# Retention and a low-rank mixer on one core: half-sequence loads of q and k, one PE burst per chunk, batch 0 from q

## The chip, the core and the metric

The kernel runs on one core of one Trainium2 chip. The core has a matrix engine (PE, with its weight loads PEld), three engines for element-wise work (DVE, ACT, POOL), and SP, which here only issues DMAs. POOL issues DMAs too, besides its own work. An engine takes its instructions in order and waits at the first one whose inputs or buffers are not free. Matmuls read SBUF and write PSUM; only DVE and ACT read PSUM here. The metric is the device time of one execution in microseconds.

## The reference

Four batches, eight heads of 64, a sequence of 768. First a decayed linear attention, then a mixer: a low-rank product along the sequence, and an MLP over the channels.

```python
for t in range(S):
    state = gamma[None, :, None, None] * state + np.einsum('bhd,bhe->bhde', k[:, :, t], v[:, :, t])
    y[:, :, t] = scale * np.einsum('bhd,bhde->bhe', q[:, :, t], state)
...
x = np.ascontiguousarray(attn_out.transpose(0, 2, 1, 3)).reshape(B, S, H * D)
...
xt = x.transpose(0, 2, 1)
h = xt @ U @ V                       # U: 768 x 32, V: 32 x 768
u = x + h.transpose(0, 2, 1)
ch = np.maximum(u @ w_ch1, 0.0) @ w_ch2   # 512 -> 2048 -> 512
return (u + ch).astype(np.float32)
```

## The kernel before

Everything on PE is bf16. The sequence of a batch is cut into six chunks of 128. The decay is folded into q and v by factors, so that a chunk needs four products: its **scores** (k by q, masked to the causal half by DVE: `a`), the **mix** (`a` by v), the **query** (q by the state of the chunks before) and the **state** (k by v, added up in PSUM). Mix and query add up in one PSUM region and give x.

The order of all instructions is written by hand. Three stages follow each other:

- **Batch 0 by itself** (L672 to L737): nothing else can run on PE yet. It works in blocks of 256 rows (`cast_early`, `turn_early`, `score_early`, `state_early`, `mix_early`), with casts shared out to DVE ("D"), POOL ("P") and ACT ("A"). Then x is turned, the low-rank product is added, and the result is written to `uTs[0]` as input of the MLP (L736).
- **Preparation of batch 1** on POOL (L738 to L755): casts of q, k, v, with the loads of the weights w1, w2 and of q's second half issued between them.
- **Three weaves** (L765 to L799): `weave` lays out the MLP of batch b-1 as a list of pieces, each with a cost in us, and calls the retention of batch b and the low-rank part at given marks, shares of that list's total. A last weave has the MLP of batch 3 alone.

An MLP piece is either `up` (L463: four matmuls of w1 with `uTs`, 512 or 256 wide, into one of three PSUM banks called mlp, then a Relu by ACT or DVE into `gT`) or `down` (L486: four of the sixteen matmuls of one output chunk; after the last, DVE adds u and POOL stores it).

Around a chunk, `score4` (L356) and `mix4` (L377) are called at two marks (L760). For b > 1 `score4` also computes the state; for b = 1 k has not been loaded in its natural layout, so `natural_k` (L319) makes it on PE, and the state comes in `mix4`. Scores and query use PE as four row tiles of 32 (shape 32*128), the state as column tiles of 32 (128*32), the rest uses it whole.

After the last chunk, `lr_proj` (L411) and `lr_expand` (L421) make u, and `lr_turn` (L436) turns it into `uTs[b]`: for b < 2 by PE (L445) and ACT, for b > 1 by DMA transposes on SP (L439), one for each chunk j. The first four must have landed before the next weave's first MLP piece.

Loads: q and k that will be turned lie in one buffer each (`kin`, `qin`), filled for batch 1 by `load_half` (head by head, half a sequence) and for batches 2, 3 by `load_whole` (L107: two heads, the whole sequence, 384 KB). k and v in natural layout (below: "naturals", 256 KB a chunk) go into a ring of 19 buffers. `feed_more` (L136) issues the loads of batches 2 and 3 on SP in list order: T (q and k whole), then k and v of each chunk, as buffers come free; `pause` (L762) stops it for a while. At most eight of SP's DMAs are under way, as each waits for the one eight places before it.

Of the kernel before, what the change touches and what calls it, by code (L numbers as in the profile page):

```python
# [16 lines left out]
def kernel(  # L17
# [75 lines left out]
    n_fed, n_held, hold_feed = [0], [0], [False]  # L93
    ready = {}
    turned_in = {}
    n_cast = {b: 0 for b in range(-1, B)}

    def feed_natural(nm, b, ci):
        src = {"k": k, "v": v}[nm]
        feed.append(((nm, b, ci),  # L100
                     src[b, :, ts(ci, P), :].rearrange("h p d -> p h d")))

    def open_in(nm, b):
        turned_in[nm, b] = rinT.tile([P, 2, NCK, 256], fp32, tag=nm + "in",
                                     name=f"{nm}in_{b}")

    def load_whole(nm, b):  # L107
        open_in(nm, b)
        src = {"q": q, "k": k}[nm][b]
        for hp in (0, 2, 1, 3):  # L110
            nc.sync.dma_start(
                out=turned_in[nm, b][ds(32 * hp, 32)].rearrange(
                    "p h c x -> p (h c) x"),
                in_=src[ds(2 * hp, 2)].rearrange("h (c t j) d -> t (h c) (j d)",
                                                 c=NCK, t=32))

    def load_half(nm, half, eng, part=range(8)):
        c = ds(3 * half, 3)
        src = {"q": q, "k": k, "v": v}[nm]
        if nm != "v":  # L120
            if half == 0:
                open_in(nm, 1)
            for h in [(0, 4, 1, 5, 2, 6, 3, 7)[i] for i in part]:
                eng.dma_start(
                    out=turned_in[nm, 1][ds(32 * (h // 2), 32), h % 2, c],
                    in_=src[1, h, ts(half, 384)].rearrange(
                        "(c t j) d -> t c (j d)", c=3, t=32))
            return
        for ci in range(3 * half, 3 * half + 3):
            t = rin.tile([P, 512], fp32, tag="in", name=f"v1_{ci}")  # L130
            n_held[0] += 1
            ready["v", 1, ci] = t
            eng.dma_start(out=t.rearrange("p (h d) -> p h d", h=H),
                          in_=src[1, :, ts(ci, P)].rearrange("h p d -> p h d"))

    def feed_more():  # L136
        while n_fed[0] < len(feed) and n_held[0] < RING and not hold_feed[0]:
            key, src = feed[n_fed[0]]
            if key[0] == "T" and n_cast[key[1] - 1] < 2 * NCK:
                return  # L140
            n_fed[0] += 1
            if key[0] == "T":
                load_whole("k", key[1])
                load_whole("q", key[1])
                continue
            n_held[0] += 1
            t = rin.tile([P, 512], fp32, tag="in", name=f"in_{n_fed[0]}")
            ready[key] = t
            nc.sync.dma_start(out=t.rearrange("p (h d) -> p h d", h=H), in_=src)  # L149
# [5 lines left out]
    for b in range(2, B):  # L155
        feed.append((("T", b), None))
        for ci in range(NCK):
            feed_natural("k", b, ci)
            feed_natural("v", b, ci)
    NB = S // 256  # L160
    early = {}
    kin0 = rinT.tile([P, NB, H, P], fp32, tag="kin", name="kin_0")
    qin0 = rinT.tile([P, NB, H, P], fp32, tag="qin", name="qin_0")

    def load_early(nm, B0):
        src = {"q": q, "k": k, "v": v}[nm][0, :, ds(256 * B0, 256), :].rearrange(
            "h (t j) d -> t h (j d)", j=2)
        if nm == "v":
            early["v", B0] = []
            for f in range(2):  # L170
                t = rin.tile([P, 4, P], fp32, tag="in", name=f"v0_{B0}_{f}")
                nc.sync.dma_start(out=t, in_=src[:, ds(4 * f, 4)])
                early["v", B0].append(t)
        else:
            t = (kin0 if nm == "k" else qin0)[:, B0]
            nc.sync.dma_start(out=t, in_=src)
            early[nm, B0] = t

    for nm, B0 in ("k0", "q0", "v0", "k1", "q1", "v1", "q2", "k2", "v2"):
        load_early(nm, int(B0))  # L180
# [45 lines left out]
    def late_consts():  # L226
        nc.vector.tensor_scalar(mask, jmat, srange, None, op0=ALU.is_ge)
        nc.vector.tensor_tensor(
            pos, pos, lgt[:, None, :].to_broadcast([P, NCK, H]), op=ALU.mult)
        nc.scalar.activation(gk, pos, AF.Exp, scale=-1.0)  # L230
        for h in range(H):
            r = ds(32 * (h // 2), 32)
            nc.vector.tensor_scalar(
                posT[r, :, h % 2], posT[r, :, h % 2],
                -0.5 * math.log(D) / lg[h] - 128.0 * (h // 2), lg[h],
                op0=ALU.add, op1=ALU.mult)
        nc.scalar.activation(gqT, posT, AF.Exp)

    def causal(n):
        return mask[:, None, :].to_broadcast([P, n, P])  # L240
# [3 lines left out]
    def prep_turned(nm, b, ci, eng="P"):  # L244
        src = turned_in[nm, b][:, :, ci].rearrange("p h (a j d) -> p h a j d", a=2,
# [86 lines left out]
    def state(b, ci):  # L332
        if ci == NCK - 1:
            return
# [17 lines left out]
        ns = rmid.tile([P, 320], bf16, tag="ns", name=f"ns_{b}_{ci}")  # L352
        evac("A", ns[:, :256], st_p[:, :256])
        live["state", b, ci] = ns

    def score4(b, ci):  # L356
        if b == 1:
            natural_k(b, ci)
# [15 lines left out]
        if b > 1:  # L374
            state(b, ci)
# [457 lines left out]
```

## Time and profile before

| what | value |
|---|---|
| median of 8 runs | 234.86 us (233.65 to 235.85) |
| profiled execution, its own time | 234.14 us |
| its span in the profile | 232.3 us |
| PE busy | 212.6 us (92%) |
| DVE, ACT, POOL busy | 106.2, 78.8, 94.7 us |
| DMA moved | 34.95 MB, mean 150 GB/s |
| MLP up matmuls (L467) | 500 recorded, 89.3 us busy |
| MLP down matmuls (L492) | 385 recorded, 85.0 us busy |

The span is the time from the first to the last instruction in the profile; the difference to the execution's own time lies around it. A line such as "A L1 <- B L2: 1.5, 1, 1.5" among the waits says that engine A, at line 1, waited for what B did at line 2: in total, how often, and the longest. A timeline row has start, length, engine, line, operation, tiles (out<-in), shapes and count; a row merges equal instructions that follow each other. A few matmul records are missing from a trace.

### The profile page before, as it was taken

To read this page: it belongs to the slowest core of one execution; us is meant where nothing else is said; L and a number is where in the kernel's file an instruction comes from. 1 tells how busy PE (TensorE), PEld (TensorE's weight loads), DVE (VectorE), ACT (ScalarE), POOL (GpSimd) and SP (SyncE) were. 2 spreads that over 40 slices of the span, in tenths; PEclk is the share of its full clock that TensorE was granted. 3 is DMA by queue.
4 is the path that set the end of the run, shared out by engine and by line. 5 is a ranking of instruction groups with operands and counts; after the bars stand their busy time and mean duration, and the time that the engine had idled before them with its cause. 6 is when DMAs were issued, how large, how long until landed. Compare 5 with 4: busy or idle time off the path is not lost.

```text
span 232.3 us, 5722 instructions
## 1 busy us (share of the span) xinstructions
PE 212.6 (92%) x2402; PEld 119.4 (51%) x2430; DVE 106.2 (46%) x200; ACT 78.8 (34%) x173; POOL 94.7 (41%) x132
## 2 busy tenths in 40 slices
PE   0589699999999999999999979999999999999991
PEld 0478445657445444467444424477444444774451
DVE  5267558665534254555435155555436152222121
ACT  2474355567212127456210025555110044540000
POOL 3787159897111499911098176400101100001110
PEclk9999999999999999999999999999999999999999
DMA  7999989999999999099999932000022530001212
GB/s 180 290 291 245 232 195 224 277 208 195 235 206 215 314 235 275 24 218 205 189 242 251 254 76 45 3 1 3 3 90 71 158 90 0 3 0 47 92 62 74
DMA packets 63882, 34.95 MB, mean 150 GB/s; under 512 B 40064, under 2 KB 61952, under 8 KB 63856
## 3 DMA queue, kind: packets, MB, share of 16 engines
q1 hardware_dynamic: 57344, 23.37, 48.4%
q0 software_dynamic: 6512, 11.21, 19.9%
q8 instruction: 19, 0.31, 0.6%
q14 instruction: 7, 0.06, 0.1%
HBM read 30.90 MB, written 6.29 MB: 160 GB/s over the span
## 4 chain that ended last, share of the span: by engine, by line
PE 67%; SPq 12%; issue 9%; DMA 4%; DVE 3%; ACT 2%; POOL 1%; POOLq 0%; DVEq 0%
PE mlp L467 33%; PE mlp L492 19%; SPq L149 10%; DMA qin<-in_q_dram 2%; SPq L439 2%; PE r L396 2%; PE r L363 2%; PE mlp L566 2%; DMA uT<-u 2%; PE r L387 1%; PE st L348 1%; ACT qt L72 1%; PE r L588 1%; POOL out_dram L456 1%; PE r L424 1%
## 5 line engine op out<-in xcount | busy, mean ns | idle before, releaser
L467 PE MATMUL mlp<-uT,w1b 128*128 128x256 bf16 (+1 forms) x500 | 89.3, 325 | 2.9 <-DMA uT<-u 1.5
L492 PE MATMUL mlp<-w2b,gT 128*128 128x512 bf16 (+2 forms) x385 | 85.0, 370 | 1.0 <-issue 0.3
L474 ACT ACTIVATE gT<-mlp 128x512 bf16<-128x512 f32 (+1 forms) x88 | 42.7, 490 | 75.8 <-PE mlp L467 74.9
L467 PEld LDWEIGHTS <-w1b 128*128 128x128 bf16 x512 | 47.6, 98 | 33.3 <-issue 3.6
L492 PEld LDWEIGHTS <-gT 128*128 128x128 bf16 x400 | 37.2, 98 | 40.6 <-issue 0.2
L456 POOL DMA_DIRECT2D out_dram<-o x24 | 13.3, 555 | 94.4 <-DVE o L499 94.4
L499 DVE TENSOR_TENSOR o<-mlp,u 128x512 f32<-128x512 f32 (+2 forms) x25 | 16.8, 670 | 47.8 <-PE mlp L492 44.4
L472 DVE TENSOR_SCALAR gT<-mlp 128x512 bf16<-128x512 f32 (+1 forms) x40 | 22.0, 550 | 29.6 <-PE mlp L467 29.6
L369 DVE TENSOR_TENSOR a<-r,mask 128x512 bf16<-128x512 f32 x36 | 23.2, 685 | 19.4 <-PE r L363 14.5
L85 POOL TENSOR_TENSOR qi<-qin,gqT 128x512 bf16<-128x512 f32 x18 | 18.9, 1051 | 9.8 <-DMA qin<-in_q_dram 9.7
L72 ACT ACTIVATE x<-r 128x256 bf16<-128x256 f32 x36 | 11.8, 382 | 20.6 <-PE r L396 20.4
L83 POOL CAST ki<-kin 128x512 bf16<-128x512 f32 x18 | 13.8, 767 | 11.3 <-DVE gT L472 7.2
L431 DVE TENSOR_TENSOR u<-r,x 128x512 bf16<-128x512 f32 (+1 forms) x16 | 14.5, 951 | 4.2 <-PE r L424 3.6
L85 POOL TENSOR_TENSOR vd<-in,gk 128x512 bf16<-128x512 f32 x12 | 12.5, 1039 | 3.6 <-PE r L396 3.2
L72 ACT ACTIVATE uT<-r 128x1024 bf16<-128x1024 f32 (+1 forms) x6 | 5.2, 880 | 12.0 <-PE r L445 9.7
L593 DVE TENSOR_TENSOR a<-r,mask 128x1024 bf16<-128x1024 f32 x6 | 7.1, 1220 | 4.1 <-PE r L588 3.9
L566 PE MATMUL mlp<-ident,kb 128*128 128x128 bf16 x24 | 3.1, 312 | 5.6 <-DVE kb L83 5.6
L363 PE MATMUL r<-qT,kT 32*128 32x128 bf16 x288 | 7.5, 217 | 0.5 <-DVE u L431 0.5
L313 DVE STREAM_TRANSPOSE kT<-ki 128x256 f32<-128x256 f32 x18 | 7.8, 436 | 0.0
L313 DVE STREAM_TRANSPOSE qT<-qi 128x256 f32<-128x256 f32 x18 | 7.3, 408 | 0.9 <-POOL qi L85 0.9
L83 POOL CAST kd<-in 128x512 bf16<-128x512 f32 x12 | 7.3, 609 | 1.0 <-POOL qi L85 0.9
L85 POOL TENSOR_TENSOR vd<-v,gk 128x512 bf16<-128x512 f32 x6 | 6.3, 1056 | 2.8 <-DMA v<-in_v_dram 2.8
(79 smaller groups left out, 138.7 us busy)
## 6 DMA issues: line engine op xcount, KB each, us to landing
out_dram<-o POOLq DMA_DIRECT2D x23, 256.0 KB, 3.2
v<-in_v_dram SPq DMA_DIRECT2D x12, 256.0 KB, 7.0
kin<-in_k_dram SPq DMA_DIRECT2D x8, 384.0 KB, 8.6
qin<-in_q_dram SPq DMA_DIRECT2D x8, 384.0 KB, 13.6
in<-in_k_dram SPq DMA_DIRECT2D x12, 256.0 KB, 5.4
in<-in_v_dram SPq DMA_DIRECT2D x12, 256.0 KB, 5.3
w1b<-in_moe_w_ch_dram POOLq DMA_DIRECT2D x4, 512.0 KB, 8.3
w2b<-in_moe_w_ch_dram POOLq DMA_DIRECT2D x4, 512.0 KB, 12.3
```

The costliest lines, as they stand in the source:

```text
L72: nc.scalar.activation(dst, src, AF.Copy)
L83: e.tensor_copy(out=dst, in_=src)
L85: e.tensor_tensor(dst, src, scale, op=ALU.mult)
L149: nc.sync.dma_start(out=t.rearrange("p (h d) -> p h d", h=H), in_=src)
L313: nc.vector.transpose(out=dst, in_=src)
L369: nc.vector.tensor_tensor(a[:, ds(4 * g, 4)].rearrange("p (n i) m -> p n i m", n=2), R[g][:, :, :256].rearrange("p n (i m) -> p n i m", i= ...
L456: nc.gpsimd.dma_start(out=dst, in_=src)
L467: nc.tensor.matmul(g_p[:, :sz], w1b[:, c, ts(m, P)], uTs[b][:, c, ds(lo, sz)], start=(c == 0), stop=(c == NCB - 1))
L472: nc.vector.tensor_relu(gT[:, m, ds(lo, sz)], g_p[:, :sz])
L474: nc.scalar.activation(gT[:, m, ds(lo, sz)], g_p[:, :sz], AF.Relu)
L492: nc.tensor.matmul(ch[:, :nn], gT[:, m, ts(j, P)], w2b[:, m, ds(n0, nn)], start=(m == 0), stop=(m == NM - 1))
L499: nc.vector.tensor_tensor(o_sb, ch[:, :nn], us[b][:, j, n], op=ALU.add)
```

## The change

- The buffers of q and k are halves now (`kin0`, `kin1`, `qin0`, `qin1`), and batches 2 and 3 are loaded head by head into them (sixteen DMAs of 96 KB for a half of q and k), as batch 1 was. The list of loads becomes: T half 0, k and v of chunks 0, 1, T half 1, k and v of the rest; `feed_more(n)` may issue n entries more. One entry is allowed at mark 0.50 of weave 1, the others after the transposes of u, eighteen at first, which ends ahead of batch 3's second half.
- `score4` and `mix4` become `burst`: mix and query of chunk n, scores of chunk n+1 and state of chunk n together, at one mark. Mix and query use columns 256 to 383 of the banks R, scores columns 0 to 255.
- u of batch 1 is turned by DMA for j 0 to 3; expand and all four transposes are issued at one mark (`spread`).
- Batch 0 begins with q: order of loads and casts, kt on DVE, q's transposes of block 1 ahead of the mix, x_turn between the halves of the last mix, uT evicted in halves of 256 and the first MLP pieces 256 wide, half of the last v cast on DVE, `late_consts` on POOL with its two exps on ACT later, q's second half of batch 1 issued in one place.

```diff
-    def load_whole(nm, b):
-        open_in(nm, b)
-        src = {"q": q, "k": k}[nm][b]
-        for hp in (0, 2, 1, 3):
...
+    def load_turned(nm, b, half, eng=None, part=range(8)):
+        eng = eng or nc.sync
...
+        for h in [(0, 4, 1, 5, 2, 6, 3, 7)[i] for i in part]:
+            eng.dma_start(out=turned_in[nm, b, half][ds(32 * (h // 2), 32), h % 2],
+                          in_=src[b, h, ts(half, HC * P)].rearrange(
+                              "(c t j) d -> t c (j d)", c=HC, t=32))
...
+    def feed_more(n=0):
+        allowed[0] += n
+        while n_fed[0] < len(feed) and n_held[0] < RING and allowed[0] > 0:
+            nm, b, i = feed[n_fed[0]]
+            if nm == "T" and n_cast[b - 1] < NCK * (i + 1):
                 return
...
     for b in range(2, B):
-        feed.append((("T", b), None))
-        for ci in range(NCK):
-            feed_natural("k", b, ci)
-            feed_natural("v", b, ci)
+        for nm, i in (("T", 0), (0, 0), (0, 1), ("T", 1), (0, 2), (0, 3), (0, 4), (0, 5)):
+            feed += [("T", b, i)] if nm else [("k", b, i), ("v", b, i)]
...
-    for nm, B0 in ("k0", "q0", "v0", "k1", "q1", "v1", "q2", "k2", "v2"):
+    for nm, B0 in ("q0", "k0", "v0", "k1", "q1", "v1", "q2", "k2", "v2"):
         load_early(nm, int(B0))
...
     def late_consts():
-        nc.vector.tensor_scalar(mask, jmat, srange, None, op0=ALU.is_ge)
-        nc.vector.tensor_tensor(
+        nc.gpsimd.tensor_scalar(mask, jmat, srange, None, op0=ALU.is_ge)
+        nc.gpsimd.tensor_tensor(
...
+    def burst(b, n):
+        m = n + 1
+        mix, score = n >= 0, m < NCK
+        if score and b == 1:
+            natural_k(b, m)
+        if mix:
+            vb, a = pre["v", b, n], live.pop(("a", b, n))
+            for g in range(2):
+                for i in range(2):
+                    for hp in (2 * g, 2 * g + 1):
+                        nc.tensor.matmul(R[g][:, hp % 2, ds(256 + D * i, D)],
+                                         a[:, 2 * hp + i], vb[:, 2 * hp + i],
...
+        if n > 0:
+            st = live.pop(("state", b, n - 1))
...
+                        nc.tensor.matmul(R[hp // 2][:, hp % 2, ds(256 + D * i, D)],
+                                         turned("qT", b, n, i, c, r),
+                                         st[r, ts(2 * i + c, D)], start=False,
...
+        if score:
...
+                        nc.tensor.matmul(R[hp // 2][:, hp % 2, ts(i, P)],
+                                         turned("kT", b, m, i, c, r),
+                                         turned("qT", b, m, i, c, r),
...
+        if mix and score:
+            state(b, n)
...
+        for g in range(2):
+            if mix:
+                evac("A", four(xs[b][:, n])[:, ds(2 * g, 2)], R[g][:, :, ds(256, P)])
+            if score:
+                nc.vector.tensor_tensor(
...
+        if mix and score:
+            ns = rmid.tile([P, 320], bf16, tag="ns", name=f"ns_{b}_{n}")
+            evac("A", ns[:, :256], live["st_p", b][:, :256])
...
     def lr_turn(b, j0):
-        if b > 1:
+        if b > 1 or (b == 1 and j0 < 4):
             for j in (j0, j0 + 1):
...
         run = NM // 2 if b == 0 else NM
+        if b == 0:
+            for lo in (0, 256):
+                pieces += [(0.432, up(m, lo, 256)) for m in range(4)]
...
+    cast_early("q", 0, ("D", 0, 4), ("P", 6, 2), ("D", 4, 2))
+    turn_early("q", 0)
     cast_early("k", 0, ("D", 0, 4), ("D", 4, 4))
-    turn_early("k", 0)
-    cast_early("q", 0, ("P", 6, 2), ("D", 0, 6))
-    turn_early("q", 0)
+    turn_early("k", 0, "D")
...
     cast_early("q", 1, ("P", 4, 4), ("D", 0, 4))
+    open_mix(0)
+    turn_early("q", 1, "D")
     mix_early(0)
-    turn_early("q", 1, "D")
...
-    cast_early("v", 2, ("P", 0, 4), ("P", 4, 4))
+    cast_early("v", 2, ("P", 0, 4), ("D", 4, 4))
...
     cast_uv("v")
+    late_consts()
...
-    fill(2)
-    for c in range(NCB):
-        evac("AD"[c // 2], uTs[0][:, c, :LO], xT(c)[:, :LO])
-    late_consts()
-    n_cast[0] = 2 * NCK
-    feed_more()
+    fill(1)
+    for lo in range(2):
+        for g in range(2):
+            evac("AD"[g], uTs[0][:, ds(2 * g, 2), ts(lo, 256)], R[g][:, :, ts(lo, 256)])
+    late_exps()
...
     load_w1(3)
-    load_half("q", 1, nc.gpsimd, range(6))
     prep_natural("v", 1, 0)
     prep_chunk(1, 1)
-    load_half("q", 1, nc.gpsimd, range(6, 8))
+    load_turned("q", 1, 1, nc.gpsimd)
     load_w2(0)
     load_w2(1)
...
-    AT = {1: [(a, a + 0.042) for a in (0.19, 0.26, 0.33, 0.40, 0.465, 0.53)], 2: at(0.09, 0.105, 0.05)}
-    LR = {1: (0.62, 0.66, 0.72, 0.78), 2: (0.69, 0.73, 0.80, 0.86)}
-    def pause():
-        hold_feed[0] = True
+    AT = {1: (0.20, 0.265, 0.33, 0.40, 0.465, 0.53, 0.575),
+          2: [0.085 + 0.095 * i for i in range(NCK)] + [0.63]}
+    LR = {1: (0.62, 0.66), 2: (0.67, 0.71)}
...
-            marks = [(0.03, part(lr_expand, 0, 4, 2)), (0.10, part(lr_turn, 0, 4)),
-                     (0.16, part(lr_expand, 0, 0, 4))]
+            marks = [(0.075, part(lr_expand, 0, 4, 2)), (0.125, part(lr_turn, 0, 4)),
+                     (0.15, part(lr_expand, 0, 0, 4)), (0.50, part(feed_more, 1))]
...
+        def spread():
+            lr_expand(b, 0, 4)
+            lr_turn(b, 0)
             lr_turn(b, 2)
-            hold_feed[0] = False
-            feed_more()
-        marks += zip(LR[w], (mixed, part(lr_expand, b, 0, 4), part(lr_turn, b, 0),
-                             last_turn))
+            feed_more(18 if b == 1 else len(feed))
+        marks += zip(LR[w], (mixed, spread))
```

## The prediction, on record before the changed kernel ran

> **What bounds the kernel now.** I read the page first, then the waits, the chain, the timeline of PE around one chunk, and last the landings of single DMAs. The page:
>
> ```profile
> span 232.3 us, 5722 instructions
> PE   0589699999999999999999979999999999999991
> DMA  7999989999999999099999932000022530001212
> ```
>
> Each digit is 5.8 us. PE is full from slice 5 on but for one slice near 134 us, and the DMA engines are full too until about 90 us. So up to 90 us two things can set the pace; after that only PE does. What stops PE at 134 us stands in the waits and the chain:
>
> ```profile
> PE mlp L467 <- DMA uT<-u: 1.5, 1, 1.5
> ```
>
> ```profile
> 130.09 1.64 SPq L439
> 131.78 3.58 DMA uT<-u
> 135.37 0.25 issue
> 135.61 0.59 PE mlp L467 x2
> ```
>
> The next MLP cannot start until the fourth DMA transpose of u of batch 2 has landed (135.37). The timeline of PE around one chunk, with start, length and count:
>
> ```profile
> 91.03 0.40 PE L396 MATMUL r<-vd,a 128*128 128x64 bf16 x8
> 91.26 2.75 PE L467 MATMUL mlp<-uT,w1b 128*128 128x512 bf16 x12
> 93.94 0.40 PE L363 MATMUL r<-qT,kT 32*128 32x128 bf16 x16
> 94.28 0.30 PE L348 MATMUL st<-vd,kd 128*32 128x64 bf16 x16
> 94.51 1.90 PE L467 MATMUL mlp<-uT,w1b 128*128 128x512 bf16 x7
> 96.34 0.30 PE L387 MATMUL r<-ns,qT 32*128 32x64 bf16 x16
> ```
>
> Read the starts. Twelve MLP matmuls take 2.59 in the chain (0.216 each), yet the scores start 2.68 after them: 0.09 is lost where the tile changes from 128*128 to 32*128. Single starts show the same step at each change of tile: 0.312 for 0.216, 0.144 for 0.057, 0.126 for 0.029. L396, full-size, follows L467 or precedes it without a step.
>
> Where data sets the pace: POOL's first cast of batch 1 waits for its load, and the last load of w2 (issued at 48.9) lands at 48.9 + 16.6 = 65.5, only 1.2 us before PE reaches its first use (the down matmul of m0=12, at 66.65).
>
> ```profile
> POOL ki L83 <- DMA qin<-in_q_dram: 4.1, 1, 4.1
> ```
>
> ```profile
> L296 POOL DMA_DIRECT2D w2b<-in_moe_w_ch_dram x4: 760/795/808, 43.9 to 48.9; - x4
> DMA to landing us min/median/max: 9.9/12.3/16.6
> ```
>
> **The change, part by part.** I call the stretch with the MLP of batch b-1 and the retention of batch b "weave b". They ran from 28.7 to 83.5, to 135.6, to 185.8; the last MLP ends the span.
>
> *One burst per chunk.* The matmuls stay the same; only changes of tile go. Before, a middle chunk of batches 2, 3 has five (MLP to scores, to state, to MLP, to query, to mix), the first three, the last four: 27. A burst goes mix, query, scores, state, MLP, and query and scores share a tile: three changes in bursts 0 to 4, two in the opening and the closing one: 19. Saved: 8 x 0.095 = 0.76 us each for batches 2 and 3. In batch 1 state followed mix, so 32 changes become 19: 13 x 0.095 = 1.24 us. Against it: ACT's evictions (x 0.35 twice, state 0.39, in batch 1 kn 0.6) and DVE's masks (0.65 twice) now come in one heap of up to 1.7 us, while a 256-wide MLP piece takes 0.44 and has three banks. After the two bursts of a batch that lie among such pieces, PE may wait 0 to 0.25 us for a bank: 0 to 1.5 in all; I take 0.4, since two of three pieces' evictions fit ahead of the heap's end.
>
> *u of batch 1 turned by DMA.* 16 L445 matmuls at 0.056 go from PE: 0.89 us. Four transposes go to SP after u (DVE's end near 71.5): issues of 1.3 each, the last landing about 6.4 after the first issue (batch 3: 178.03 to 184.42), so 78, before the next MLP at 82. Hidden; uncovered it would cost what lies past 82.
>
> *Loads held behind the transposes of u.* SP's queue in the new program is: first half of q, k, transposes of j 0 to 3, k and v of two chunks, second half, the other k, v. For batch 3 the transposes stand behind its first half and four naturals, which end near 112, and u is there near 123, so the transposes wait for u alone. From expand to last landing took 9.4 us in batch 3 (174.98 to 184.42); at mark 0.71 expand comes 11.5 before the next MLP. The wait goes: 1.84 between the two matmuls around it, less one step of 0.216, is 1.62 us saved. With the contended pace of before (126.78 to 135.37, 8.6 for 6.4) it would be 0.2 late.
>
> What is late instead: q, k of chunks 3 to 5 and k, v from chunk 2 on. Behind the batch 1 transposes (issued to 77) stand four naturals to 81, sixteen half loads to 88.6 (SP's spacing 0.47), then k of chunk 2, landing near 92. On POOL, stores, kd, vd and the casts of chunk 3 stand behind it: kd and vd to 94.1, store, ki and qi (0.76, 1.04) to 96.4, DVE's turns to 97.3. Scores of chunk 3 come 18.9 us into weave 2, at 101. Spare: 3.9 us. It becomes a stall from there on.
>
> *Halves per head.* A load of 384 KB (L111) lands every 1.92 us when alone (101.02, 102.95, 104.87, 106.79); 96 KB ones (L124) land every 0.29 (eight from 31.00 to 33.00). So a batch's q, k cost 32 x 0.29 = 9.3 us of DMA instead of 8 x 1.92 = 15.4. A rule speaks against it: the Trainium skill, "DMA: Bandwidth & Descriptors", section "Rules for kernel authors", wants many small transfers merged into one large one, and its section on the anatomy of a DMA (on GpSimd's path) has about 2 us fixed for each. By that, 24 more DMAs a batch with eight in flight would cost an estimated 24 x 2 / 8 = 6 us more of queue. The landing rows say 6.1 us less, and I go by them.
>
> *Batch 0 begins with q.* q lands first (5.04), k second (6.77). ACT's 1.31 of qt then runs beside k's casts and transposes; kt goes to DVE (0.69): scores near 8.75 instead of 10.24. Then k of the next block is pinned by its load (10.39) and cast (1.17), but q's transposes of block 1 move ahead of the mix, so its scores come 1.1 earlier. The narrower evictions of uT and a half of v on DVE add up to 0.8. MLP starts at 27 to 27.6 instead of 28.7 to 29.2, worth 1.1 to 1.9. late_consts on POOL: ten small operations, between 0.13 (DVE's rows of them) and 0.35 (CAST of 192) each, 1.3 to 3.5 us from 26.56, under POOL's wait for its load, which ends at 30.6; ACT's exps behind them can hold the first MLP pieces about 1 us.
>
> *Does that start survive weave 1?* PE would reach burst 1 (scores of chunk 2) 17.6 after the start, about 44.9. Its kT needs POOL: vd of chunk 1 waits for v landing at 38.80 and ends at 39.85; then, new there, all eight q loads are issued at 0.55 to 0.58 (six stood before it), to 44.3; two w2 loads, to 45.9; ki to 46.6, DVE's turn to 47.1; qi and its turn to 48.1. So PE waits 2.2 us at 44.9 and leaves burst 1 near 48.8, where before the same work was done at 48.63. All of the early gain, and more, goes into a wait for POOL, which waits for loads. The price of that wait is the start's own gain: without it weave 1 would end 2.2 earlier. After the 1.46 wait at 134 us the pitch was 0.216 as ever, so I add nothing for the clock. The Trainium skill, "TensorE: Matmul & The Clock Gate", Part 1, has PE at half clock after an idle window of some 3.4 us, for about as long: were the wait to grow past that, an estimated 1.7 us would come on top.
>
> From there nine changes of tile fewer (0.86): m0=12 falls at 66.65 + 0.17 - 0.86, and counted by hand through the bursts 66.5; I take 66.2, just after w2's 65.5. Gain in weave 1: 0.45 + 0.89 = 1.3 us. At best PE is at m0=12 as w2 lands (2.0).
>
> *Sum:* 1.3 + 1.62 + 0.76 + 0.76 - 0.4 = 4.05 us. Span 232.3 - 4.05 = 228.25. The profiled run took 234.14 by itself, 1.84 around its span; the median of eight is 234.86, so 230.8.
>
> **Rivals.**
> - *Paced by PE in weave 1 after all:* loads land earlier thanks to the halves, and the start carries through: 1.4 + 1.24 + 0.89 + 1.62 + 1.52 = 6.7, 228.2. For it: POOL's issues could end sooner. Against: the DMA row is full to 65 us and no byte is saved there.
> - *The heap costs, transposes stay contended:* 1.5 instead of 0.4, and 0.2: 232.1. For it: ACT has 1.7 us at once. Against: most bursts lie among 512-wide pieces.
> - *w2 comes late (slower):* the first half of batch 2 waits only for POOL's casts of chunk 2, so it enters SP's queue near 48 and shares the engines with w2. If all sixteen pass before w2's last load at the slow pace (16 x 0.48 = 7.7, for the 1.9 of the 384 KB that did so before), w2 lands at 71.3, PE waits 5.1, and the total is 234.86 - 4.05 + 5.1 = 235.9. It decides slower once w2 lands past about 70.3. Against: v of chunk 5 holds SP's ring to 59.6 as before, and then SP had work in both.
> - *It doesn't do what it says:* only partly so: the order shows the first half ahead of the transposes, which is counted above.
>
> **Numbers.** Forecast 0.55, start carries 0.15, heap 0.15, w2 late 0.10, other 0.05. A change under 0.5% (1.2 us) can't be told from none. Faster: 0.55 + 0.15 + 0.12 = 0.82; within: 0.08 (milder w2 delay, part of heap); slower 0.10. Time 230.8; range 228.2 (start carries) to 233.8 (heap and w2 2 us late together).
>
> **What would show it.** Right: no wait for uT near 132; L387 followed by L363 without a step; no L445 in batch 1 but for j 4; PE idle about 2 us near 45 before kT of chunk 2; w2 landing by 66. Wrong: that idle time missing, several new waits of L363 or mix for POOL in weave 2, MLP pieces waiting for ACT after bursts, or w2 landing past 68.

## The result, and the profile after

The changed kernel takes 239.05 us (median of 11 runs, 236.67 to 240.22), the kernel before 234.96 (median of 32, 233.41 to 239.63): a ratio of 1.0174, 95% interval 1.0142 to 1.0206. It is 1.7% slower; 230.8 was forecast. The profiled execution took 239.33 us, 237.3 of it span. In the experiments below medians are of all executions, while ratios leave out those more than 1.5% above the fastest of the same kernel, and the profiled executions of pe45, ord45, qload and spread are of that kind.

The starts of the four MLPs cut the span into the weaves of the forecast (its 0.4 us for the heap is spread here over the three weaves). Us:

| | first MLP starts | weave 1 | weave 2 | weave 3 | last MLP | span |
|---|---|---|---|---|---|---|
| before | 28.70 | 54.84 | 52.08 | 50.00 | 46.68 | 232.3 |
| forecast | 27 to 27.6 | ends at 82.4 | 49.8 | 49.4 | 46.7 | 228.25 |
| after | 28.99 | 56.72 | 49.74 | 55.12 | 46.73 | 237.3 |

Weave 2 came out as worked out. Weave 1 ended 3.3 us later than forecast, and weave 3 took 5.7 more: those two are the whole miss. The page of the profile after (rows of 40 slices, 5.9 us each):

```profile
span 237.3 us, 5776 instructions
PE   0798897959999999999999999669999999999992
PEclk9999999979999999999999999979999999999998
DMA  7999979999933899996823759920012620001212
```

The hole of PE near 134 us is gone. There are two others: slice 8 (47 to 53 us) and slices 25 and 26 (148 to 160). The row of granted clocks falls to 7 in slices 8 and 26. From slice 26 on DMA has little to do. The waits (us in total, times, longest) name what was late:

```profile
PE mlp L452 <- DMA uT<-u: 4.1, 1, 4.1
...
PE mlp L314 <- DVE kT L302: 3.3, 2, 2.1
```

*Weave 3.* The name is that of the old wait, uT by DMA, but it is another transpose. PE's timeline (start, length, what, count, idle time before and its releaser):

```profile
149.54 0.29 PE L360 MATMUL r<-ns,qT 32*128 32x64 bf16 x16
149.67 0.39 PE L369 MATMUL r<-qT,kT 32*128 32x128 bf16 x16
149.99 0.30 PE L335 MATMUL st<-vd,kd 128*32 128x64 bf16 x16
150.22 1.90 PE L452 MATMUL mlp<-uT,w1b 128*128 128x512 bf16 x7
156.23 3.23 PE L452 MATMUL mlp<-uT,w1b 128*128 128x256 bf16 x16 [4.11 <-DMA uT<-u]
```

In the burst, query (L360) and scores (L369) follow each other without the step of 0.09, as forecast. At 156.23 the first 256-wide up pieces start, which read the last 256 columns of uT: those are chunks 4 and 5 of u of batch 2. They come from `lr_turn(2, 4)`, issued on SP. SP's timeline:

```profile
126.74 5.26 SPq L424 DMA_TRANSPOSE uT<-u  x4
132.10 3.84 SPq L107 DMA_DIRECT2D kin<-in_k_dram  x8
136.04 4.72 SPq L107 DMA_DIRECT2D qin<-in_q_dram  x8
140.81 0.43 SPq L116 DMA_DIRECT2D k<-in_k_dram  x1
...
149.03 3.71 SPq L424 DMA_TRANSPOSE uT<-u  x2
```

Between the first four transposes and the last two stand sixteen half loads and eight naturals, 16.9 us of SP. u itself was ready at 138.03, when DVE's additions for it ended (L416); the kernel before issued the same two transposes at 138.21 and 139.45. Now they land at 155.75 and 156.18.

*Weave 1.* PE's timeline around burst 1, then POOL's:

```profile
44.70 2.76 PE L452 MATMUL mlp<-uT,w1b 128*128 128x512 bf16 x11
49.60 0.40 PE L314 MATMUL mlp<-ident,kT 128*128 128x128 bf16 x4 [2.14 <-DVE kT L302]
...
50.57 0.42 PE L369 MATMUL r<-qT,kT 32*128 32x128 bf16 x16
...
52.08 4.26 PE L452 MATMUL mlp<-uT,w1b 128*128 128x512 bf16 x14 [0.22 <-issue]
```

```profile
37.57 1.03 POOL L85 TENSOR_TENSOR vd<-v,gk 128x512 bf16<-128x512 f32 x1 [2.24 <-DMA v<-in_v_dram]
...
40.25 1.03 POOL L85 TENSOR_TENSOR vd<-v,gk 128x512 bf16<-128x512 f32 x1
41.23 4.39 POOL L107 DMA_DIRECT2D qin<-in_q_dram  x8
46.78 1.52 POOL L285 DMA_DIRECT2D w2b<-in_moe_w_ch_dram  x2 [1.16 <-DMA qin<-in_q_dram]
48.28 0.78 POOL L83 CAST ki<-kin 128x512 bf16<-128x512 f32 x1
```

The forecast wait is there, 2.14 us before kT of chunk 2. But POOL comes to that cast at 48.28, not at 45.9: it waited 2.24 for v of chunk 0, which landed at 37.49 (35.20 before), and 1.16 for a q load. And the MLP behind the burst is slow: fourteen matmuls of 512 take 4.26 us (0.304 each, not 0.216), the first of them at a granted clock of one half. So is the one behind the wait of weave 3 (sixteen of 256 take 3.23). The first wait of 1.21 us in the L314 row, at 40.27, was not forecast.

### The profile page after: what moved, and what is told of

Its sections match the earlier page's. It is cut to its first block, busy times and chain, and to the rows that moved or that the text cites. A ratio compares the mean times of both kernels' runs of the same rounds, so it can differ in the third digit from the quotient of the medians.

```text
span 237.3 us, 5776 instructions
## 1 busy us (share of the span) xinstructions
PE 213.5 (90%) x2403; PEld 123.3 (52%) x2429; DVE 107.5 (45%) x194; ACT 76.0 (32%) x173; POOL 96.3 (41%) x141
## 4 chain that ended last, share of the span: by engine, by line
PE 36%; issue 32%; DMA 12%; SPq 10%; POOL 7%; DVE 1%; POOLq 0%; ACT 0%; DVEq 0%
PE mlp L452 14%; PE mlp L482 13%; DMA kin<-in_k_dram 4%; DMA v<-in_v_dram 4%; DMA u<-in_k_dram 4%; SPq L107 3%; POOL out_dram L441 3%; SPq L424 2%; SPq L163 2%; SPq L165 2%; POOL qi L85 2%; POOL vd L85 1%; SPq L116 1%; PE r L369 1%; PE r L350 1%
## 5 line engine op out<-in xcount | busy, mean ns | idle before, releaser
L452 PE MATMUL mlp<-uT,w1b 128*128 128x256 bf16 (+1 forms) x516 | 90.4, 326 | 5.4 <-DMA uT<-u 4.1
L459 ACT ACTIVATE gT<-mlp 128x256 bf16<-128x256 f32 (+1 forms) x90 | 42.9, 479 | 92.9 <-PE mlp L452 91.6
L452 PEld LDWEIGHTS <-w1b 128*128 128x128 bf16 x528 | 50.8, 100 | 37.3 <-DMA uT<-u 4.6
L482 PEld LDWEIGHTS <-gT 128*128 128x128 bf16 x400 | 37.5, 98 | 42.4 <-issue 0.4
L457 DVE TENSOR_SCALAR gT<-mlp 128x256 bf16<-128x256 f32 (+1 forms) x42 | 22.8, 545 | 26.4 <-PE mlp L452 26.4
L85 POOL TENSOR_TENSOR vd<-v,gk 128x512 bf16<-128x512 f32 x18 | 18.7, 1038 | 5.3 <-DMA v<-in_v_dram 4.7
L416 DVE TENSOR_TENSOR u<-r,x 128x512 bf16<-128x512 f32 (+1 forms) x16 | 14.6, 952 | 5.5 <-PE r L409 5.5
L83 POOL CAST kd<-k 128x512 bf16<-128x512 f32 x12 | 7.3, 606 | 19.1 <-DMA k<-in_k_dram 19.1
L555 PE MATMUL mlp<-ident,qb 128*128 128x128 bf16 x24 | 3.5, 310 | 5.9 <-DVE qb L85 5.7
L350 PEld LDWEIGHTS <-a 128*128 128x128 bf16 x144 | 6.7, 100 | 2.5
L350 PE MATMUL r<-vd,a 128*128 128x64 bf16 x144 | 7.4, 196 | 0.0
L369 PE MATMUL r<-qT,kT 32*128 32x128 bf16 x288 | 7.1, 215 | 0.1
```

The source lines that it names most:

```text
L83: e.tensor_copy(out=dst, in_=src)
L85: e.tensor_tensor(dst, src, scale, op=ALU.mult)
L350: nc.tensor.matmul(R[g][:, hp % 2, ds(256 + D * i, D)], a[:, 2 * hp + i], vb[:, 2 * hp + i], start=(i == 0), stop=True, skip_group_check=True)
L416: nc.vector.tensor_tensor(v4(us[b][:, ds(j0, nj), e]), R[g][:, :, :nj * P].rearrange("p c (j e) -> p c j e", j=nj), v4(xs[b][:, ds(j0, nj) ...
L452: nc.tensor.matmul(g_p[:, :sz], w1b[:, c, ts(m, P)], uTs[b][:, c, ds(lo, sz)], start=(c == 0), stop=(c == NCB - 1))
L457: nc.vector.tensor_relu(gT[:, m, ds(lo, sz)], g_p[:, :sz])
```

## The experiments

Every time below stands beside runs of the kernel before on the same chip, with the ratio to them where there is one. The weaves are read from each profiled execution.

| run | time, us (before) | ratio, 95% interval | profiled execution | start | weave 1 | weave 2 | weave 3 |
|---|---|---|---|---|---|---|---|
| pe45 | 234.04 (235.92) | 0.9895, 0.977 to 1.002 | 235.97 | 29.31 | 58.69 | 49.74 | 49.74 |
| ord45 | 233.16 (235.92) | 0.9912, 0.9859 to 0.9965 | 234.32 | 28.81 | 57.74 | 49.74 | 49.29 |
| turn0 | 239.18 (235.92) | 1.0186, 1.0117 to 1.0256 | 239.34 | 28.77 | 55.36 | 49.74 | 56.76 |
| qload | 243.9 (235.92) | | 244.63 | 28.90 | 60.90 | 49.74 | 56.38 |
| cast2 | 238.97 (235.34) | 1.0129, 1.007 to 1.0187 | 237.91 | 28.11 | 55.93 | 49.74 | 55.42 |
| late | 238.25 (233.81) | 1.0174, 1.0118 to 1.0229 | 238.37 | 28.28 | 56.14 | 49.74 | 55.48 |
| home | 237.74 (235.34), one run | | 237.74 | 29.12 | 54.74 | 49.74 | 55.44 |
| kfirst | 233.12 (236.09) | 0.9888, 0.9795 to 0.9981 | 233.14 | 28.20 | 57.18 | 49.74 | 49.29 |
| ordcast | 232.11 (235.34) | 0.9877, 0.9837 to 0.9917 | 232.18 | 28.51 | 55.89 | 49.74 | 49.29 |
| spread | 231.89 (235.34) | 0.9822, 0.9779 to 0.9865 | 235.43 | 28.89 | 58.81 | 49.73 | 49.29 |
| best | 231.88 (233.81) | 0.9917, 0.988 to 0.9953 | 232.67 | 28.73 | 56.17 | 49.74 | 49.29 |
| kbest | 231.71 (236.19) | 0.9881, 0.9784 to 0.9977 | 231.22 | 27.97 | 55.71 | 49.74 | 49.29 |

### Weave 3: the two transposes behind the loads

The suspected pair is taken off SP (pe45), or only moved forward in SP's queue (ord45).

```diff
-        if b > 1 or (b == 1 and j0 < 4):
+        if b > 2 or (b > 0 and j0 < 4):
```

> The changed kernel, except that chunks 4 and 5 of u of batch 2 are turned by PE (as those of batch 1 are) and not by two DMA transposes. Theory 1 (the two transposes stood on SP's queue behind sixteen half loads and eight naturals, and PE waited for them): the 4.1 us wait of the first 256-wide up pieces at 156 goes, and so does the half clock behind it (sixteen matmuls of 256 took 3.03 us at 156.23, about 1.76 at the usual 0.11, so some 1.3 to 1.5 us); eight matmuls of 0.056 come on top (0.45). Weave 3 falls from 55.1 to about 50, the time from 239.05 to 233.9. Rival (weave 3 is long because its loads and POOL are late, and the transposes only happen to land last): the wait moves to the scores of chunk 3, weave 3 stays at 53 or more, time above 237. Weave 1 stays at 56.7 in both.

```diff
+        order = [("T", 0), (0, 0), (0, 1), ("T", 1), (0, 2), (0, 3), (0, 4), (0, 5)]
+        if b == 3:
+            order[3:5] = order[4], order[3]
...
-                     (0.06, part(lr_turn, b - 1, 4))]
+                     (0.06 if b == 2 else 0.025, part(lr_turn, b - 1, 4))]
+            if b == 3:
+                marks.append((0.03, part(feed_more, len(feed))))
...
-            feed_more(18 if b == 1 else len(feed))
+            feed_more(18 if b == 1 else 2 if b == 2 else len(feed))
```

> The changed kernel with another order on SP's queue alone: after the transposes of chunks 0 to 3 of u of batch 2 only k and v of chunk 2 of batch 3 are issued, then the two transposes of chunks 4 and 5 (mark 0.025 of the next weave), and the second half of q, k and the other six naturals behind them. Theory 1: transposes land near 143, the 4.1 us wait and the 1.3 to 1.5 us of half clock go, nothing is added on PE: weave 3 about 49.5, time 233.5. What could come instead: q and k of the second half land about 10 us later than now (near 150) and the scores of chunk 3, due about 154, wait up to 2 us. Rival (contention, not order): the transposes still land past 152.

Measured: weave 3 falls from 55.12 to 49.74 (pe45) and 49.29 (ord45). The difference of the two is 0.45, the eight matmuls of 0.056 that pe45 adds. SP's timeline of ord45:

```profile
127.58 5.26 SPq L427 DMA_TRANSPOSE uT<-u  x4
132.89 0.58 SPq L116 DMA_DIRECT2D k<-in_k_dram  x1
133.51 0.58 SPq L116 DMA_DIRECT2D v<-in_v_dram  x1
138.89 2.89 SPq L427 DMA_TRANSPOSE uT<-u  x2
141.89 3.83 SPq L107 DMA_DIRECT2D kin<-in_k_dram  x8
```

The transposes are issued at 138.89, where the kernel before had them, and land by 143.28. The loads that went behind them keep no one waiting. No byte and no operation differs from the changed kernel; only the order on one queue does. So 55.12 - 49.29 = 5.83 us of weave 3 are that order: 4.11 of wait, and 1.7 of half clock behind it. All eight profiles with the mended order show 49.29. The rival (late loads, contention) falls. Weave 1, expected to stay at 56.7, took 58.69 and 57.74: it varies without an edit, of which more below.

### Weave 1: POOL's order, DVE's order, or the bytes

turn0 puts DVE's turns of chunk 0 ahead of the two additions of u (L416, 2.35 us at 37.52) that stood before them.

```diff
-            marks.append((at - 0.6 * step, part(turn_chunk, b, ci)))
+            marks.append((0.145 if (b, ci) == (1, 0) else at - 0.6 * step,
+                          part(turn_chunk, b, ci)))
```

> The changed kernel with DVE's turns of k and q of chunk 0 of batch 1 put ahead of the expansion of u (mark 0.145 instead of 0.161; DVE's two additions of u, 2.35 us, now stand behind them). Theory 2a (the 1.21 us wait at 40.3 is DVE's order, an effect of where the expansion now sits): that wait falls to 0 to 0.5, since the scores still need R from the additions. If POOL pins chunk 2 (kT at 49.1 whatever PE did before), the gain is lost again in the wait at 49.6, which grows from 2.1 to about 3: time 238.5 to 239.5, no change. Rival (PE's own work sets weave 1): weave 1 falls by 0.7 to 1.2 and the time to 238.

The first wait falls from 1.21 to 0.5, and the second grows from 2.14 to 3.12: PE comes earlier to a burst that POOL holds. The 1.21 was DVE's order, and cost nothing while the next wait stood behind it. Weave 1 is 1.4 shorter all the same, because no half clock followed this wait (more on that below), and weave 3 is 1.6 longer, because its wait was 4.87 and two periods of half clock came with it; the time is unchanged.

qload puts back where POOL issues q's second half.

```diff
     load_w1(3)
+    load_turned("q", 1, 1, nc.gpsimd, range(6))
     prep_natural("v", 1, 0)
     prep_chunk(1, 1)
-    load_turned("q", 1, 1, nc.gpsimd)
+    load_turned("q", 1, 1, nc.gpsimd, range(6, 8))
```

> The changed kernel with the second half of q of batch 1 issued on POOL where it was before: six loads ahead of v of chunk 0, two after chunk 1. Theory 2 (the 2.14 us wait at 49.6 is for POOL, which issued all eight loads, 4.4 us, and then waited 1.2 for a place in its queue before it cast k of chunk 2): kT of chunk 2 comes near 46.5 instead of 49.1, the wait goes, and with it the wait for qT (0.4) and the half clock behind it (fifteen matmuls of 512 took 4.9 us for 3.3, 1.6): weave 1 from 56.7 to 52.5, unless w2, which lands near 66, holds it (then 53.3); time 235 to 236. The 1.21 us wait at 40.3 stays. Rival (the data are late, not POOL's order): kT of chunk 2 still comes after 48.5, weave 1 stays at 56 or more, time 238.5 to 239.5. The wait of 4.1 at 156 stays in both.

In the profiled execution this missed: kT of chunk 2 comes hardly earlier (PE goes on at 48.99, not 46.5), and three more waits of 1.07 to 1.54 us follow before 69. POOL, ahead of its last q load, now waits 2.98 us for the last w1, which landed at 45.28 (43.04 before the change). But that profile is of an execution of 244.63; another took 236.53, close to the 235 to 236 of theory 2, and has no profile. So the old place alone does not bring the old weave back every time, and between theory 2 and its rival qload does not decide.

cast2 leaves the loads together and puts the casts ahead of them that have their data.

```diff
     prep_chunk(1, 1)
+    prep_turned("k", 1, 2)
+    prep_turned("q", 1, 2)
     load_turned("q", 1, 1, nc.gpsimd)
...
-    prep_chunk(1, 2)
+    prep_natural("v", 1, 2)
```

> The changed kernel with POOL's casts of k and q of chunk 2 of batch 1 put ahead of its eight loads of q and two of w2 (their data landed by 33); the loads are issued 1.75 us later. Theory 2b (the wait for kT of chunk 2 is POOL's queue: casts that have their data stand behind loads, which stand behind landings): kT of chunk 2 comes near 44 instead of 49, the wait of 2.1 to 4.2 at 47.5 goes, and no half clock follows it near 50. But the loads are now later: chunk 3 of batch 1 (second half of q) is cast near 54, so the scores of chunk 3, due near 52, wait about 2 us. Weave 1 from 56.7 to 53.5 to 55.5, time 236 to 238. Rival (weave 1 is paced by bytes, whatever the order of POOL): the whole wait reappears at chunk 3, weave 1 stays at 56 or more, time 238.5 or more. The 1.2 us wait at 40 and the 4.1 at 156 stay.

The wait at burst 1 is gone (46.78, no idle time before it), and with it the half clock; at chunk 3 the wait is 0.62, not 2. Yet weave 1 takes 55.93, between the two expectations, and the time moves little (236.95 to 240.03 in three executions; a fourth of 1173.67 pulls the median up by 1). PE's timeline shows what took the place:

```profile
65.95 0.52 PE L400 MATMUL r<-x,Ub 128*32 128x128 bf16 x24
68.06 1.89 PE L482 MATMUL mlp<-w2b,gT 128*128 128x512 bf16 x7 [1.59 <-DMA w2b<-in_moe_w_ch_dram]
```

PE now reaches m0=12 before the last w2, which lands at 68.02 (66.20 after the change, 65.47 before it). In this kernel it was POOL's order that made PE wait at burst 1; behind that wait stands w2.

A likely reason that w2 lands later, though it is issued 2 us earlier (49.68 for 51.74), lies in other loads. The early casts also free the buffers for the first half of q and k of batch 2, whose sixteen loads SP now issues from 46.43 and not from 49.09. All sixteen land ahead of the last w2, where six did. The profiles of changed kernels fall into two groups here (spread aside, whose last w2 is issued at 57.43). In nine, v of chunk 5 lands at 59.16 or later, at most six of the sixteen land ahead of the last w2, and that w2 takes 13.31 to 14.83 us from issue to landing. In five (pe45, cast2, ordcast, best, kbest) v of chunk 5 lands by 54.11, all sixteen come first, and w2 takes 16.15 to 18.76. So w2 seems to share the DMA engines with loads that nothing needs before weave 2. That is inferred from the groups: the kernel before has 14.31 to 16.58 with loads of another size, and no run holds the loads of batch 2 back.

late gives PE 2 us more of MLP ahead of each burst of weave 1.

```diff
-    AT = {1: (0.20, 0.265, 0.33, 0.40, 0.465, 0.53, 0.575),
+    AT = {1: (0.245, 0.31, 0.375, 0.445, 0.51, 0.575, 0.62),
```

> The changed kernel with all bursts of weave 1 put 0.045 of the weave later (about 2 us of MLP pieces stand ahead of each). Theory 2c (weave 1 is long because PE reaches its bursts before POOL and the loads have their q and k, and a wait there also brings half clock): the 1.2 us at 40 goes, the wait at burst 1 (0.5 to 4.2 in the runs so far) falls by 2, half clock only if more than 1.5 us is left; weave 1 from 54.7 to 58.7 so far to 52.7 to 54, time 235 to 236, with the wait at 156 still in it. Rival (bytes pace the weave to its end: w2 and v of chunk 5 come when they come): PE only waits later, for w2 near 66 or v near 65, weave 1 stays at 55.5 or more and the time at 238 to 239.

The wait of 1.21 goes, but one of 1.89 stays at 47.45, with half clock behind it, and weave 1 takes 56.14. Weave and time are those of the rival, though the waits that it named (for w2 and v) did not come; the ratio is that of the changed kernel.

### The beginning with q

home asks whether k of block 2 is late because of the tile that it lands in.

```diff
-    for nm, t in (("k", us[1]), ("q", uTs[1])):
+    for nm, t in (("q", us[1]), ("k", uTs[1])):
```

> The changed kernel with the two borrowed homes of block 2 of batch 0 swapped: k into the tile of uT, q into that of u. k of block 2 landed at 19.05 (17.59 before the change), which put its transposes at 19.87 and ate the early start. If the tile in which it lands is at fault, q lands near 17.3 and k by 17.7 to 18, and the first MLP starts near 28. If it is the load's place in the queue, k still lands near 19 and the MLP starts at 28.8 to 29.3. Weave 3 keeps its wait.

k lands at 19.13 again: not the tile. It tells something else: four profiles share the code of weave 1 (the changed kernel, pe45, ord45, home), and kT of chunk 2 held PE for 2.14, 4.17, 3.11 and 0.50 us in them. POOL came to the cast that this wait is for at 48.28, 50.61, 49.07 and 46.78. Ahead of its loads it had waited for v of chunk 0 in the first (landed at 37.49) and for v of chunk 1 in the others (43.68, 39.79 and 37.83). The same instructions, loads that land up to 6 us apart.

kfirst is ord45 with batch 0 beginning with k.

```diff
-    for nm, B0 in ("q0", "k0", "v0", "k1", "q1", "v1", "q2", "k2", "v2"):
+    for nm, B0 in ("k0", "q0", "v0", "k1", "q1", "v1", "q2", "k2", "v2"):
...
-    cast_early("q", 0, ("D", 0, 4), ("P", 6, 2), ("D", 4, 2))
-    turn_early("q", 0)
     cast_early("k", 0, ("D", 0, 4), ("D", 4, 4))
-    turn_early("k", 0, "D")
+    turn_early("k", 0)
+    cast_early("q", 0, ("P", 6, 2), ("D", 0, 4), ("D", 4, 2))
+    turn_early("q", 0)
...
     open_mix(0)
-    turn_early("q", 1, "D")
     mix_early(0)
+    turn_early("q", 1, "D")
```

> The run ord45 (changed kernel, SP's order mended) with batch 0 beginning with k again: load order, the casts and turns of block 0, and q's turn of block 1 behind the mix, all as before the change. What is tested: whether beginning with q is what brings the loads of weave 1 in late (v of chunk 2 landed at 42.4 to 45.2 in five runs of the changed code up to there, 39.7 and 41.2 before the change; the last w1 at 44.1 to 44.5 against 42.6 and 43.0). If so: v of chunk 2 by 41.5, last w1 by 43.2, the wait at burst 1 under 1 us, weave 1 54 to 54.7 instead of 57.7, time 230.5. If the late loads come from elsewhere in the change (q's second half all issued in one place on POOL, the held order), they land as late as now, k of block 2 still lands near 19, weave 1 56 to 58 and the time 232 to 234. The first MLP starts at 28.7 to 29.2 in both.

k of block 2 lands at 17.64, v of chunk 2 of batch 1 at 39.74, the last w1 at 43.50, and the MLP starts at 28.20, earlier than in the kernel that begins with q. The wait at burst 1 is still 2.54 us, since POOL's order is as in the changed kernel; weave 1 takes 57.18 and the time is that of ord45. So loads that land as early as before the change do not bring weave 1 back while POOL's order stays. The kernel before was profiled again too, and kfirst twice more:

> The kernel before, unchanged, profiled once more: how much does its weave 1 vary from run to run? With the changed kernel's code unchanged up to there, weave 1 took 56.7, 58.7, 57.7, 55.4 in four runs. If the change made weave 1 sensitive (theory 2), before's stays within 54.3 to 55.3 and its MLP shows no wait over 0.6 us between 40 and 66; if the loads vary by themselves, it shows such a wait too.

> The run kfirst once more, for one profile. In the kernels that begin with q, k of block 2 landed late (18.7 to 19.2) in 9 of 12 profiles, and in just those v of chunk 2 of batch 1 landed late too (42.4 to 46.9 for 39.7 to 41.2); in the three that begin with k never. If beginning with q is the cause: k of block 2 by 17.7 and v of chunk 2 by 41.3 again. If it is a state of the run that has nothing to do with the order, about three of four such profiles show 18.7 or later.

> As kfirst_b: k of block 2 by 17.7 if the order of q and k is the cause, 18.7 to 19.2 in three of four profiles if it is not.

> The kernel before once more, for one profile: k of block 2 by 17.7 and v of chunk 2 by 41.3 if the order is the cause; 18.7 or later in three of four if it is a state of the run.

| | before2 | before3 | kfirst_b | kfirst_c |
|---|---|---|---|---|
| time, one run | 233.66 | 235.56 | 235.15 | 230.89 |
| k of block 2 lands | 17.68 | 17.58 | 18.03 | 17.54 |
| v of chunk 2 lands | 39.74 | 41.55 | 44.66 | 40.15 |
| first MLP | 28.45 | 28.09 | 28.32 | 27.81 |
| weave 1 | 54.98 | 56.31 | 59.01 | 55.54 |

k of block 2 lands between 17.53 and 18.03 in all seven profiles that begin with k (these, kfirst, kbest and the first of the kernel before), and at 18.69 or later in eight of the eleven that begin with q (the expectations' count of nine in twelve was one too high): the order brings it late, though not always. The first MLP starts at 27.81 to 28.70 with k first (28.2 on average), at 28.11 to 29.31 with q first (28.8); in the three of these in which k was early it starts at 28.11, 28.28 and 28.51. But v of chunk 2 is late (44.66) in kfirst_b, where k is not, so the late loads of weave 1 are not explained by that order alone. before2 has no wait over 0.6 between 40 and 66, but before3 shows that the kernel before varies as well: weave 1 of 56.31, with 1.04 us of wait near 64.

### Versions put together

ordcast is ord45, turn0 and cast2 at once.

> Three edits at once: the order of SP's queue of the run ord45, the turns of chunk 0 ahead of the expansion (run turn0) and the casts of chunk 2 ahead of the loads (run cast2). If they add: start 28.9, weave 1 54, weave 2 49.74, weave 3 49.3, last MLP 46.7, so a span of 228.6 and a time near 230.3, 2% under before. If the loads pace weave 1 it stays at 55 to 56.5 and the time at 231.5 to 233.

spread also moves six q loads and the casts of chunk 3 forward (the latter not shown) and puts the release of the first half of batch 2 at a later mark:

```diff
     prep_natural("v", 1, 0)
+    load_turned("q", 1, 1, nc.gpsimd, range(6))
     prep_chunk(1, 1)
+    prep_turned("k", 1, 2)
+    prep_turned("q", 1, 2)
+    load_turned("q", 1, 1, nc.gpsimd, range(6, 8))
...
-(0.50, part(feed_more, 1))
+(0.60, part(feed_more, 1))
```

> As ordcast, but six of the eight loads of q go ahead of chunk 1's casts, the casts of k, q of chunk 3 ahead of v of chunk 2 and the last w2 loads, and the first half of batch 2 is released at mark 0.60 of weave 1 instead of 0.50, so that it doesn't share the engines with w2. If POOL's order is what holds weave 1: no wait of PE over 0.6 us between 40 and 66, w2 landed by 65, weave 1 53 or less, time 229 to 230. If the early q loads push v or w1 back (as in the run qload, where the last w1 landed at 45.3 and the weave took 60.9), weave 1 is 56 or more, time above 232.

best is ordcast with that later mark and with `AT[1]` at 0.20, 0.28, 0.355, 0.43, 0.495, 0.555, 0.595; kbest is ordcast beginning with k.

> The three edits of the run ordcast, the bursts of weave 1 later by 0 to 0.03, and the first half of batch 2 released at mark 0.60 instead of 0.50. If waits and half clock are what is left in weave 1 (1.2, 0.5, 0.5 and about 1.5 in the run ordcast): weave 1 52.5 to 53.5, span 227.5, time 229 to 230, over 2% under before. If loads pace it: weave 1 stays near 55.5, time 231.5 to 232.5.

> The run ordcast (SP's order, turns of chunk 0 ahead of the expansion, casts of chunk 2 ahead of the loads) with batch 0 beginning with k. If late loads from beginning with q are what is left of weave 1's loss: MLP from 28.2, weave 1 54, span 227.9 to 229, time 229.5 to 231. If bytes pace it: weave 1 stays at 55.9 and the end of the span at 229.9, time 231.7.

All four beat both kernels, by 0.8 to 1.8% against the one before with intervals that stay below 1, and no median reached the time that the better case of its expectation gave. What weave 3 gets back is kept. In the four profiles weave 1 takes 55.7 to 58.8 whichever wait is taken away: ordcast waits 1.20 for kT of chunk 3, spread 3.90, best 1.46 for qT of chunk 3 and then 0.63 and 1.28 for w2, kbest 0.72 and 0.80 for kT and qT of chunk 3 and 0.45 for w2. In three of the four the second case (the loads pace it) held to its numbers.

Two limits of this. The later mark of best did not hold the loads of batch 2 back. SP issued them as early as in ordcast (47.62), while PE came to the burst of mark 0.43 only at 52.20:

```profile
46.85 6.84 SPq L107 DMA_DIRECT2D kin<-in_k_dram  x8
55.31 6.84 SPq L107 DMA_DIRECT2D qin<-in_q_dram  x8
```

A mark gives an instruction its place in SP's order, but SP does not wait there for PE. So best does not test whether these loads hold w2 up. And spread's profile is of an execution of 235.43, while another took 229.92 and has no profile. Weaves 2 and 3 and the last MLP are the same to 0.02 us in all eight profiles with the mended order, so start and weave 1 together must have been some 5.5 us shorter in that one, an estimate from the two times: weave 1 can be near 53, and no trace shows what differs then.

## Why the forecast was wrong, step by step

- **One burst per chunk: right, with the heap at 0.05 a weave instead of 0.13 (0.4 in all).** Weave 3 with the order mended is 49.29: 50.00 - 0.76 = 49.24 was the sum without the heap. Weave 2 says the same with the wait taken out: 52.08 - 1.62 - 0.76 = 49.70 against 49.74.
- **The wait for uT at 134: right.** Gone in every profile of a changed kernel. In the two further profiles of the kernel before it was 1.12 and 2.06, so the 1.62 was one draw of something between 1.3 and 2.2.
- **u of batch 1 by DMA: right.** The last transpose landed at 81.19, the MLP needed it at 85.71.
- **Loads of batch 2 behind the transposes: right.** No wait for chunk 3; weave 2 is 49.74 to 0.01 in all fifteen profiles with the changed queue.
- **Loads of batch 3 behind the transposes: the step that failed.** Of batch 3 the forecast said that "the transposes wait for u alone", which held for j 0 to 3. But its list of SP's queue ("first half of q, k, transposes of j 0 to 3, k and v of two chunks, second half, the other k, v") stops one entry too early. The transposes of j 4 and 5 of the u of batch 2 are issued one weave later and come behind everything that the release lets through. For batch 1 that does not matter, as PE turns j 4 and 5 there; so what holds for the MLP of weave 2 does not hold for that of weave 3. Price: 5.83 us, most of the miss.
- **Weave 1, the wait before burst 1: the mechanism right, its length right by luck.** 2.2 was forecast, 2.14 found, but at 47.5 to 49.6 and not at 44.9 to 47.1, for both sides came some 2.5 later. PE did, as it started at 28.99 and not at 27.3 and waited 1.21 on the way. POOL did, as v of chunk 0 landed at 37.49, so that its loads began 1.4 later, and as it waited 1.16 for a q load to land before it could issue w2. The sum left such waits out, though POOL's rows of before have one (0.88 us, for a w1, ahead of the last q load). The forecast's burst ended near 48.8; the MLP went on at 51.3. With 1.6 of half clock behind it, m0=12 came at 69.72 and not at 66.2.
- **"I add nothing for the clock": wrong.** 1.7 us in weave 3 (within the 5.83), and 1.6 in weave 1 (fifteen matmuls of 512 from 51.26 to 56.18: 4.92 us for 15 x 0.216 + 0.09).
- **Beginning with q: wrong in sign.** 1.1 to 1.9 us earlier was forecast; 0.3 later came out (28.8 against 28.2 over all profiles), and the late k of block 2 is not all of it: where k was early, the start was only as with k first. It had no part in the sum, since the forecast lost it in weave 1 anyway.
- **PE's saving in weave 1: right, and lost in the profiled executions.** Without its waits weave 1 takes 54.32 before the change (54.84 - 0.52) and 52.05 in kfirst_c (55.54 - 1.21 - 2.28): 2.3 less, 2.13 were forecast for tiles and transposes. The waits take it back: before the change the last w2 came 1.2 us ahead of its use already, and POOL's queue and w2 held PE in turn.
- **Halves per head: no gain seen.** 0.29 us a load was read from eight landings between 31.00 and 33.00, but those loads had been issued from 26.20 to 30.75, 0.65 apart. In weaves 2 and 3 of the changed kernel sixteen of them land 0.46 to 0.55 apart (from 83.98, 101.22 and 132.10 on), so a batch's 32 take an estimated 15 to 18 us, where the forecast had 9.3, and 15.4 for the old kind. The term was not in the sum, and nothing in weaves 2 and 3 waits for these loads.

Of the rivals, w2 late came nearest in kind. It did not happen in the changed kernel (w2 landed at 66.20, its first use was at 69.7), but w2 holds PE in cast2, best and kbest, and the first half of batch 2, which that rival named, lands along with it. What stays open is why v of chunk 1 lands up to 6 us apart in runs of the same code, and v of chunk 2 later than before the change (42.4 to 45.2 in the four of that code, 39.7 to 41.6 before): that the loads share the DMA engines differently from run to run is only inferred.

## What to carry to other kernels

When loads are held behind an event and then released at once, write down the whole queue to the end of the program: whatever is issued later on that queue, however small, now waits for all of them. Check a step worked out for one iteration against what the next one does differently (here PE or DMA for the last two chunks). A place in the order of an engine that waits for nothing does not delay what stands there. And saving work of an engine in a stretch whose loads land just in time turns into waits, which may cost clock on top.

## What the runs showed of the clock

The forecast held a wait of under 3.4 us to be free of clock loss. The profiles show a fixed grid. In the changed kernel the granted clock falls at 50.83 and again at 156.65, 31 x 3.413 us apart, and each time for one such period. The windows of that grid (from:to, length, then PE's busy time; PEclk is the third value from the end), changed kernel:

```profile
47.42:50.83 3.41, 1.16 (x45) 0.93 (x44) 1.21 (x3) 0.60 (x1) 3.41 (x5) 1.00 1.24 205
50.83:54.25 3.42, 3.20 (x35) 1.32 (x25) 2.00 (x4) 1.53 (x4) 3.42 (x6) 0.50 1.22 204
```

and turn0, whose wait was longer (3.12 us, 46.53 to 49.65):

```profile
44.86:48.27 3.41, 1.67 (x8) 0.59 (x6) 0.49 (x1) 1.18 (x2) 1.49 (x3) 1.00 1.16 220
48.27:51.69 3.42, 1.87 (x62) 1.38 (x64) 1.68 (x4) 1.23 (x4) 3.42 (x5) 1.00 1.26 210
51.69:55.10 3.41, 3.41 (x26) 1.76 (x25) 2.29 (x5) 1.74 (x5) 3.41 (x5) 1.00 1.22 199
```

In the changed kernel 2.14 us fall into one window, PE is busy for 1.16 of it, and the next window runs at half clock. In turn0 the border cuts 3.12 us in two, 1.67 and 1.87 stay busy, and the clock stays whole. So it is the share of a period that counts, not the length of a wait: 1.41 busy of 3.41 brought half clock (late), 1.77 did not (cast2). Near there it is not clean: 1.66 in ord45 and 1.89 in kbest brought it too, and 1.57 in pe45 did not (46.21 to 49.62), so the profile's busy time alone does not decide it. The Trainium skill, "TensorE: Matmul & The Clock Gate", Part 1, has a free-running window of 3.413 us, which these edges agree with; it speaks of an idle window, and here a third busy was idle enough.
